# Query sketches and numerators of the later chunks in 32x32 tiles, in an attention and GELU kernel

## The chip, the core and the metric

The kernel runs on one core of a Trainium2 chip. The metric is the device time of one launch in microseconds (us): 259.41 us, the median of three runs from 259.04 to 259.57.

## What is computed

Polysketch attention (4 batches, 4 heads, 1088 tokens, head width 32) feeds a feed-forward layer with exact GELU. All in float32; `moe_w_in` and `moe_w_out` come as float64.

```python
def phi(x):                                   # S1, S2: (8, 32)
    a = np.einsum('rd,bhsd->bhsr', S1, x)
    b = np.einsum('rd,bhsd->bhsr', S2, x)
    return np.einsum('bhsi,bhsj->bhsij', a, b).reshape(*x.shape[:-1], r * r)   # 64 features
q_p, k_p = phi(q), phi(k)
kv = np.einsum('bhsf,bhsd->bhfd', k_p, v)
z = np.sum(k_p, axis=2)
num = np.einsum('bhsf,bhfd->bhsd', q_p, kv)
den = np.einsum('bhsf,bhf->bhs', q_p, z)[..., None] + 1e-06
x = (num / den)                               # then (B*S, H*D) = (4352, 128)
h = x @ w_in                                  # (4352, 2048)
out = (0.5 * h * (1 + erf(h / sqrt(2)))) @ w_out
```

## The kernel before

**Chunks.** The 1088 tokens of a batch are two chunks of 512 and a remainder of 64. Chunks 0 to 7 are the full ones (`n // 2` is the batch), and chunk 8 holds the four remainders, 256 tokens. For each chunk the attention output stands as `xT` (128 channels by 512 tokens). From it PE (TensorE) makes 16 blocks of hidden channels (`hidden`, L721), ACT (ScalarE) applies GELU (L728), and PE multiplies with `w_out`: most of it in `two_products` (L807), a seven-product scheme whose sums of tokens POOL (GpSimd) makes; some directly in `project` (L858, L855).

**Order.** The order is written out by hand. A table of steps `t` has one hidden block per step (16 per full chunk; chunk `n` begins at `t = 16 n`); `at(t, f, ...)` puts a piece of attention into a step, and within a step an engine does its instructions in the order of the text. Chunk `n`'s query is sketched at the step before chunk `n - 1`'s hidden blocks begin, and its numerators are made one chunk later, at the step before its own hidden blocks begin. Chunks 6, 7 and 8 go together at the end (`last_sketches`, `last_attends`).

**The query path of chunks 2 to 8** (chunks 0 and 1 go another way and are not changed):

- `query_turn` (DVE, VectorE) turns the query so that partitions are head and channel: `qT`.
- `query_sketch` (L578) multiplies `qT` with the sketch matrices on PE. `S_abc[b]` holds, for a batch, four columns of `S1`, four of the sketch of `z` and eight of `S2`, for each of two heads. One product contracts 64 rows (two heads, with zeros in the foreign part of the weights), has 32 columns of weights and streams 256 tokens. Eight products make a chunk: two pairs of heads (row groups of 64), two halves of the features and two halves of the tokens (four column groups of 32).
- `query_outer` (DVE, L590 to L613) turns the result in 32x32 blocks, adds up the denominator, which lies in two groups of partitions (four reductions at L601 swap them), takes its reciprocal, multiplies out the 64 features and turns them back: `q_pT`.
- `attend_products` (L633): numerators, 64 features by 32 channels, eight products of 256 tokens. `kz[b]` holds key-times-value of batch `b`, twice, once for each half of the partitions.
- `take_x` (ACT, L644): one copy of the numerators to `xT`.

**The key path of a batch.** `features_of_all` (L977) and `outer_of_all` make key features, `add_tokens` sums them; `z_sum` and `kv_sum` (both L437) multiply on PE; `fold_z` puts the sketch of `z` into `S_abc` (DVE, L492 to L495); `turn_kv` (L467) turns key-times-value with a product for each half of the partitions, and ACT copies it to `kz` (L468). `repeat_first_z` and `turn_first_kv` do the same for batch 0, whose copy for the remainder is `kz_first` (L503).

**PSUM.** The pool `wps` has two buffers of two banks (`w_ps`). `work_banks()` takes one buffer, and a piece that takes one waits for the last use of what stood there. In `sketch_and_attend` a sketch and numerators share a pair and the key features have the other; in `kv_and_attend` and `last_sketches` the pieces take pairs one after the other.

**DMA.** All loads and nearly all stores are issued from one queue, SP's, in the order of the text: the loads, `q_rem` (L128, 16 transfers) last, then the stores of the output (L878, L884).

Of the kernel before, what the change touches and what calls it, by code (L numbers as in the profile page):

```python
# [16 lines left out]
def kernel(  # L17
# [210 lines left out]
    kz = [big.tile([128, 128], FP, name=f"kz{b}") for b in range(B)]  # L228

    kz_first = big.tile([128, 128], FP, name="kz_first")  # L230
# [218 lines left out]
    def z_sum(b):  # L449

        held["z"] = work_bank()
        for h in range(H):
            kv_product(held["z"], ones, k_s[b][:, h], h, 0, start=True, stop=True)
# [10 lines left out]
    def turn_kv(b, banks):  # L464

        for rows in (slice(0, 64), slice(64, 128)):
            pe.matmul(banks[rows, 1, :128], lhsT=kv_T[b], rhs=ident, start=True, stop=True)  # L467
        act.copy(out=kz[b], in_=banks[:, 1, :128])  # L468
# [3 lines left out]
    S_abc = [big.tile([128, 2, 2, 2 * R], FP, name=f"S_abc{b}") for b in range(B)]  # L472
    own_r = big.tile([128, 2], FP, name="own_r")

    def spread_sketches():

        pool.tensor_add(out=own_r, in0=mask4[:, 0:2], in1=mask4[:, 2:4])
        own = own_r[:, None, :, None]
        w = S_abc[0]
        pool.memset(w, 0.0)  # L480
        pool.tensor_mul(out=w[:, :, :, 0:4], in0=sT[:, 0:R].rearrange("p (i f) -> p i f", i=2)[:, :, None].broadcast_to([128, 2, 2, 4]),
                        in1=own.broadcast_to([128, 2, 2, 4]))
        pool.tensor_mul(out=w[:, :, :, R:], in0=sT[:, None, None, R:].broadcast_to([128, 2, 2, R]),
                        in1=own.broadcast_to([128, 2, 2, R]))
        pool.tensor_mul(out=S_ab, in0=sT[:, None].broadcast_to([128, 2, 2 * R]), in1=own_r[:, :, None].broadcast_to([128, 2, 2 * R]))
        for b in range(1, B):
            pool.tensor_copy(out=S_abc[b], in_=w)

    def sketch_of_z(b, ps, at):

        zs = att.tile([128, R, R], FP, name="z_s")
        dve.tensor_mul(out=zs, in0=ps[:, at:at + F].rearrange("p (i j) -> p i j", i=R), in1=sT[:, None, R:].broadcast_to([128, R, R]))  # L492
        c = ps[:, 2 * F:2 * F + R]
        dve.tensor_reduce(out=c, in_=zs, axis=mybir.AxisListType.X, op=AX.add)
        dve.tensor_mul(out=S_abc[b][:, :, :, 4:8], in0=c.rearrange("p (i f) -> p i f", i=2)[:, :, None].broadcast_to([128, 2, 2, 4]),  # L495
                       in1=own_r[:, None, :, None].broadcast_to([128, 2, 2, 4]))

    def repeat_first_z():

        of = kz[0].rearrange("f (r x) -> f r x", r=2)  # L500
        to = kz_first.rearrange("f (c r d) -> f c r d", c=NP, r=2)
        for c in range(NP):
            act.copy(out=to[:F, c], in_=of[c * F:(c + 1) * F, :, 0:D])  # L503
# [57 lines left out]
    def batch_of(n, s, i):  # L561
        return n // NCH if n < NMAIN else i * 2 + s
# [3 lines left out]
    def query_sketch(n, ps=None, tok=None):  # L566

        ps = work_banks() if ps is None else ps
        W = width[n]
        tok = ps[:, :, CW // 2:] if tok is None else tok  # L570
        m = 1 if n < NMAIN else B // 2
        N = W // 2 // m
        for s in range(2):
            for i in range(m):
                for fh in range(2):
                    for c in range(NP):
                        rows, q4 = slice(c * 64, (c + 1) * 64), 2 * s + fh
                        pe.matmul(ps[q4 * 32:(q4 + 1) * 32, c, i * N:(i + 1) * N],  # L578
                                  lhsT=S_abc[batch_of(n, s, i)][rows, fh].rearrange("p r x -> p (r x)"),
                                  rhs=qT[n].rearrange("p h j t -> p (h j t)")[rows, (s * m + i) * N:(s * m + i + 1) * N],  # L580
                                  start=True, stop=True)
        sketched[n] = ps, tok

    def query_outer(n):

        W = width[n]
        K, H2 = W // 16, W // 2
        ps, tok = sketched.pop(n)
        tok = tok[:, :, :H2]
        dve.transpose(out=tok, in_=ps[:, :, :H2])  # L590
        x = tok.rearrange("p c (k x) -> p c k x", x=2 * R)
        a, b = x[:, :, :, 0:4], x[:, :, :, 8:16]
        m = att.tile([128, 32, 4], FP, name="q_ac")[:, :K]
        den = att.tile([128, 32], FP, name="q_den")[:, :K]
        by_c = lambda t: t.rearrange("p (c k) i -> p c k i", c=NP)
        dve.tensor_copy(out=by_c(m), in_=x[:, :, :, 4:8])
        dve.tensor_mul(out=by_c(m), in0=a, in1=by_c(m))
        part = ps[:, 0, :K]
        dve.tensor_reduce(out=part, in_=m, axis=mybir.AxisListType.X, op=AX.add)
        for g in range(4):  # L600
            dve.tensor_reduce(out=den[(g ^ 1) * 32:((g ^ 1) + 1) * 32], in_=m[g * 32:(g + 1) * 32], axis=mybir.AxisListType.X,  # L601
                              op=AX.add)
        dve.scalar_tensor_tensor(out=den, in0=part, scalar=1e-6, in1=den, op0=AX.add, op1=AX.add)
        dve.reciprocal(out=den, in_=den)
        dve.tensor_mul(out=by_c(m), in0=a,
                       in1=den.rearrange("p (c k) -> p c k", c=NP)[:, :, :, None].broadcast_to([128, NP, K // 2, 4]))
        feat = att.tile([128, 2 * CW], FP, name="q_f", bufs=1)[:, :2 * W]
        qp[n] = att.tile([128, 2, W], FP, name="q_pT" if n < NMAIN else "q_pT_rem", bufs=2 if n < NMAIN else 1)
        for c in range(NP):
            dve.tensor_mul(out=feat[:, c * W:(c + 1) * W].rearrange("p (k i j) -> p k i j", i=4, j=R),  # L610
                           in0=by_c(m)[:, c, :, :, None].broadcast_to([128, K // 2, 4, R]),
                           in1=b[:, c, :, None, :].broadcast_to([128, K // 2, 4, R]))
# [4 lines left out]
    def attend(n, banks=None):  # L617
        attend_products(n, banks)
        take_x(n)

    def attend_products(n, banks=None):


        W = width[n]
        m = 1 if n < NMAIN else B // 2
        banks = work_banks() if banks is None else banks
        f = qp[n].rearrange("f r x -> f (r x)")[:, :2 * W].rearrange("f (c i n r t) -> f c i n r t", c=NP, i=m, r=2, t=32)
        N = W // 2 // m
        for i in range(m):
            for s in range(2):  # L630
                rows, b = slice(s * 64, (s + 1) * 64), batch_of(n, s, i)
                for h in range(H):
                    pe.matmul(banks[h * D:(h + 1) * D, s, i * N:(i + 1) * N],  # L633
                              lhsT=(kz[b] if b else kz_first)[rows, h * D:(h + 1) * D],
                              rhs=f[rows, h // 2, i, :, h % 2], start=True, stop=True)
        numerators_in[n] = banks

    def take_x(n):

        W, banks, m = width[n], numerators_in.pop(n), 1 if n < NMAIN else B // 2  # L640
        xT[n] = att.tile([128, CW], FP, name="xT", bufs=3)
        to = xT[n][:, :W]
        to = to.rearrange("p (s x) -> p s x", s=2) if m == 1 else to.rearrange("p (s t i) -> p s i t", s=2, i=m)
        act.copy(out=to, in_=banks[:, :, :W // 2] if m == 1 else banks[:, :, :W // 2].rearrange("p s (i t) -> p s i t", i=m))  # L644
# [326 lines left out]
    def features_of_all(b):  # L971

        ps = work_banks()
        for g in range(4):
            for c in range(NP):
                rows = slice(c * 64, (c + 1) * 64)
                pe.matmul(ps[g * 32:(g + 1) * 32, c, :CW // 2], lhsT=S_ab[rows].rearrange("p r x -> p (r x)"),  # L977
                          rhs=kT[g // 2][rows, g % 2 * 256:(g % 2 + 1) * 256], start=True, stop=True)
        held["keys"] = ps

    def outer_of_all(b):

        ps = held["keys"]
        tok = ps[:, :, CW // 2:]
        dve.transpose(out=tok, in_=ps[:, :, :CW // 2])
# [11 lines left out]
    def add_tokens(b):  # L997

        sums = held["keys"][:, :, :2 * F]
# [11 lines left out]
    def sketch_and_attend(n):  # L1011

        ps = work_banks()
        query_sketch(n, ps)
        attend(n - 1, ps[:, :, CW // 2:])

    def last_sketches(b):

        z_sum(b)
        fold_z(b)  # L1020
        banks = work_banks()
        kv = banks[:, 1, CW // 2 + 128:]
        kv_sum(b, kv)
        attend_products(NMAIN - 3, banks)
        query_sketch(NMAIN, banks[:, :, CW // 2:], banks)
        take_x(NMAIN - 3)
        take_kv(b, kv)
        two = work_banks()
        query_sketch(NMAIN - 2, two, banks)
        query_sketch(NMAIN - 1, two[:, :, CW // 2:], two)  # L1030
        query_outer(NMAIN)

    def last_attends():

        banks = work_banks()
        attend_products(NMAIN - 2, banks)
        attend_products(NMAIN - 1, banks[:, :, CW // 2:])
        attend_products(NMAIN)
# [9 lines left out]

    def kv_and_attend(b, n):

        banks = held["kv"] = work_banks()
        kv_sum(b, banks[:, 1, CW // 2:])
        if n >= NCH:
            attend(n, banks)
        take_kv(b, banks[:, 1, CW // 2:])
# [17 lines left out]
    at(16, features_of_all, 1)  # L1073
# [6 lines left out]
    at(24, z_sum, 1)  # L1080
    at(24, fold_z, 1)
    at(23, query_turn, 3)
    at(24, kv_and_attend, 1, 1)
    at(24, query_sketch, 2)
# [6 lines left out]
    for n in range(3, NCHUNK):  # L1091
# [4 lines left out]
        if n == NMAIN - 2:  # L1096
# [5 lines left out]
            at(t + 11, lambda b=b: turn_kv(b, work_banks()))  # L1102
# [5 lines left out]
        if keys:  # L1108
            at(t - 1, sketch_and_attend, n)
            at(t - 1, features_of_all, b)  # L1110
        else:
            if n % 2 == 0 and b < B:
                at(t - 1, z_sum, b)
                at(t - 1, fold_z, b)
# [139 lines left out]
```

## Time and profile before

| | |
|---|---|
| median of three runs | 259.41 us (259.04 to 259.57) |
| profiled execution, first to last instruction (span) | 257.9 us |
| granted TensorE clock, mean | 0.999 |
| L721, hidden products (64 or 128 columns of weights) | 514 passes, 136.9 us busy |
| L807, output products | 784 passes |
| L578 sketches, 256 columns / 64 columns | 96 / 32 passes |
| L633 numerators, 256 columns / 64 columns | 96 / 32 passes |
| DVE, one query step L590 to L613 (pack at 57.40) | 6.4 us |
| ACT, one copy to `xT` (L644, 128x512) | 0.59 us |

The profile is one execution, so durations are set against its span; the time of that execution is not listed by itself, and the median of the runs lies 1.5 us above the span. In a row of the timeline the first number is the start in us from the first instruction, the second the length, then engine, line of the kernel, operation, tiles (out<-in), shape and count. A float32 matmul stands in the trace as two passes, so a count of 16 is eight matmuls. In brackets stands how long the engine had been idle and what released it. The ends of matmuls are modelled, so starts are the safer number.

### The profile page before, as it was taken

What the parts mean: (1) busy time and instruction counts of PE and PEld (TensorE: products, weight loads), DVE (VectorE), ACT (ScalarE), POOL (GpSimd) and SP (SyncE); (2) the same over time, 40 slices, a digit from 0 to 9 for tenths busy, and PEclk for the clock granted to TensorE, in tenths of its full rate; (3) what the DMA queues carried; (4) which work ended last, traced back from release to release, by engine and by line L of the source; (5) the groups of instructions that cost most, each with busy time, mean ns of one, the idle gap of its engine ahead of it and who ended that gap; (6) DMA issues with size and microseconds to landing.
All of it is one profiled execution on the core that took longest, in us unless ns stands there. A gap on an engine that the chain in (4) does not pass through costs nothing.

```text
span 257.9 us, 5770 instructions
## 1 busy us (share of the span) xinstructions
PE 253.1 (98%) x2335; PEld 135.5 (53%) x2335; DVE 151.1 (59%) x313; ACT 115.2 (45%) x224; POOL 163.6 (63%) x173
## 2 busy tenths in 40 slices
PE   8989999999999999999999999999999999999995
PEld 7846444354444545444444455455544444445794
DVE  3786888969699997590178986399307000700330
ACT  4665777433626332543335332533444334433442
POOL 3313006799968778587758775787758777877300
PEclk9999999999999999999999999999999999999999
DMA  6459747751000101102000002000200200020020
GB/s 203 143 156 375 181 117 174 211 131 15 4 0 13 29 3 23 20 8 35 3 0 3 0 10 37 0 1 3 41 3 5 38 0 1 7 36 0 3 41 20
DMA packets 29594, 13.48 MB, mean 52 GB/s; under 512 B 21888, under 2 KB 27776, under 8 KB 29568
## 3 DMA queue, kind: packets, MB, share of 16 engines
q1 hardware_dynamic: 29392, 13.05, 20.2%
q8 instruction: 18, 0.29, 0.5%
q10 hardware_dynamic: 176, 0.07, 0.1%
q14 instruction: 8, 0.07, 0.1%
HBM read 10.88 MB, written 2.23 MB: 51 GB/s over the span
## 4 chain that ended last, share of the span: by engine, by line
PE 93%; SPq 2%; DMA 2%; DVE 1%; issue 0%; ACT 0%
PE h_ps L721 45%; PE o_ps L807 33%; PE o_ps L858 5%; PE w_ps L855 3%; DMA small<-in_moe_w_in_dram 2%; PE w_ps L437 1%; PE w_ps L578 1%; PE w_ps L633 1%; SPq L132 1%; PE h_ps L737 1%; SPq L100 1%; PE w_ps L977 1%; PE w_ps L656 0%; SPq L118 0%; PE w_ps L467 0%
## 5 line engine op out<-in xcount | busy, mean ns | idle before, releaser
L721 PE MATMUL h_ps<-xT,w_in 128*64 128x512 f32 (+3 forms) x514 | 136.9, 576 | 0.0
L728 ACT ACTIVATE block<-h_ps 128x512 f32<-128x512 f32 (+1 forms) x128 | 73.1, 571 | 117.2 <-PE h_ps L721 115.3
L721 PEld LDWEIGHTS h_ps<-xT,w_in 128*64 128x64 f32 (+1 forms) x514 | 41.9, 142 | 30.5 <-issue 11.6
L807 PE MATMUL o_ps<-block,w_out 128*64 128x256 f32 x224 | 57.5, 379 | 0.0
L772 POOL TENSOR_TENSOR bits_low<-block 128x512 f32<-128x512 f32 x28 | 36.0, 1286 | 27.7 <-ACT block L728 27.7
L807 PEld LDWEIGHTS o_ps<-block,w_out 128*64 128x64 f32 x224 | 30.5, 137 | 38.0 <-issue 27.5
L773 POOL TENSOR_TENSOR bits_a<-block 128x512 f32<-128x512 f32 x28 | 35.8, 1278 | 11.8 <-ACT block L728 11.8
L822 DVE COPY sums<-o_ps 64x256 f32<-64x256 f32 x8 | 3.3, 417 | 60.6 <-PE o_ps L807 60.6
L774 POOL TENSOR_TENSOR bits_e<-bits_a,block 128x512 f32<-128x512 f32 x28 | 36.1, 1288 | 2.2
L775 POOL TENSOR_TENSOR bits_m<-block,bits_e 128x512 f32<-128x512 f32 x28 | 35.9, 1282 | 2.2
L807 PE MATMUL o_ps<-bits_a,small 128*64 128x256 f32 x112 | 28.8, 379 | 0.0
L807 PE MATMUL o_ps<-bits_low,small 128*64 128x256 f32 x112 | 28.8, 379 | 0.0
L807 PE MATMUL o_ps<-block,small 128*64 128x256 f32 x112 | 28.8, 379 | 0.0
L807 PE MATMUL o_ps<-bits_m,w_out 128*64 128x256 f32 x112 | 28.7, 379 | 0.0
L807 PEld LDWEIGHTS o_ps<-block,small 128*64 128x64 f32 x112 | 15.2, 137 | 17.9 <-issue 10.8
L807 PE MATMUL o_ps<-bits_e,small 128*64 128x256 f32 x112 | 17.0, 383 | 0.0
L858 PE MATMUL o_ps<-g,w_out 128*128 128x512 f32 (+1 forms) x34 | 16.5, 572 | 0.0
L807 PEld LDWEIGHTS o_ps<-bits_m,w_out 128*64 128x64 f32 x112 | 15.3, 137 | 0.0
L807 PEld LDWEIGHTS o_ps<-bits_a,small 128*64 128x64 f32 x112 | 15.2, 137 | 0.0
L807 PEld LDWEIGHTS o_ps<-bits_low,small 128*64 128x64 f32 x112 | 15.2, 137 | 0.0
L590 DVE STREAM_TRANSPOSE w_ps<-w_ps 128x512 f32<-128x512 f32 (+1 forms) x7 | 4.8, 687 | 17.1 <-ACT xT L644 12.7
L807 PEld LDWEIGHTS o_ps<-bits_e,small 128*64 128x64 f32 x112 | 7.7, 137 | 10.6 <-issue 8.8
(195 smaller groups left out, 303.7 us busy)
## 6 DMA issues: line engine op xcount, KB each, us to landing
block<-in_moe_w_in_dram SPq DMA_DIRECT2D x3, 512.0 KB, 11.3
block<-in_moe_w_out_dram SPq DMA_DIRECT2D x3, 512.0 KB, 14.7
k<-in_k_dram SPq DMA_DIRECT2D x12, 128.0 KB, 2.9
v<-in_v_dram SPq DMA_DIRECT2D x12, 128.0 KB, 3.5
q<-in_q_dram SPq DMA_DIRECT2D x24, 64.0 KB, 2.1
out_dram<-oT SPq DMA_DIRECT2D x21, 64.0 KB, 2.2
k<-in_k_dram SPq DMA_DIRECT2D x2, 256.0 KB, 2.8
q<-in_q_dram SPq DMA_DIRECT2D x2, 256.0 KB, 3.9
```

The lines of the kernel that those rows point to most:

```text
L100: eng.dma_start(out=main[n, b][:, heads], in_=src_of[n][b, heads, 0:MAIN, :].rearrange("h (p j) d -> p h j d", j=J))
L590: dve.transpose(out=tok, in_=ps[:, :, :H2])
L721: pe.matmul(ps[rows, :W], lhsT=w[:, rows], rhs=xT[n][:, :W], start=True, stop=True)
L728: act.activation(out=g_of[n, fi][:, :W], in_=ps[:, :W], func=ACT.Gelu)
L772: pool.tensor_sub(out=s[3], in0=a11, in1=a21)
L773: pool.tensor_add(out=s[1], in0=a21, in1=a22)
L774: pool.tensor_sub(out=s[2], in0=s[1], in1=a11)
L775: pool.tensor_sub(out=s[4], in0=a12, in1=s[2])
L807: pe.matmul(acc[n][bank][half * 64:(half + 1) * 64, col:col + HW], lhsT=fixed, rhs=moving, start=opens and e == 0 and name in "4715", stop ...
L822: dve.tensor_copy(out=N[lo, 0, one], in_=a0[lo, one])
L855: pe.matmul(o_of[n][i][:, :128], lhsT=g[:, i * 128:(i + 1) * 128], rhs=w_tile(w_out_sb, fi), start=first, stop=final)
L858: pe.matmul(o_of[n][:, cols], lhsT=w_tile(w_out_sb, fi), rhs=g[:, cols], start=first, stop=final)
```

## The change

A sketch product now contracts the 32 rows of one head, with the weights `S_acb[b]` (128x32: eight columns of `S1`, eight for the sketch of `z`, eight of `S2`, eight of zeros), and streams a quarter of the tokens: 16 products of 128 columns, head by row group and token quarter by column group, each head into a bank of its own. So all 64 features of a token come out on the same partitions; the denominator is one reduction, and `query_outer` loses the four reductions, the zeros and a multiplication. A head's 64 features then lie in two blocks of 32 (`i`), so the numerators are 32 products of 128 columns that add up in pairs. `kz[b]` is `[128, 2, 128]`: `turn_kv` makes one product, ACT copies its two halves to the first 32 partitions, and three DMAs on SP spread them to the other three groups. `take_x` makes two copies, one for each pair of banks. Sketch, numerators and key features (or `z`, key-times-value and its turned form) now share four banks that are taken together.

The core of the diff (changed names in calls, and the remainder's index forms in part, left out):

```diff
-    def turn_kv(b, banks):
-        for rows in (slice(0, 64), slice(64, 128)):
-            pe.matmul(banks[rows, 1, :128], lhsT=kv_T[b], rhs=ident, start=True, stop=True)
-        act.copy(out=kz[b], in_=banks[:, 1, :128])
+    def turn_kv(b, ps):
+        pe.matmul(ps[:F, :128], lhsT=kv_T[b], rhs=ident, start=True, stop=True)
+        for i in range(2):
+            act.copy(out=kz[b][:32, i], in_=ps[i * 32:(i + 1) * 32, :128])
+        for g in range(1, G):
+            sp.dma_start(out=kz[b][g * 32:(g + 1) * 32], in_=kz[b][:32])
...
-    S_abc = [big.tile([128, 2, 2, 2 * R], FP, name=f"S_abc{b}") for b in range(B)]
+    S_acb = [big.tile([128, 4 * R], FP, name=f"S_acb{b}") for b in range(B)]
...
     def repeat_first_z():
...
         for c in range(NP):
-            act.copy(out=to[:F, c], in_=of[c * F:(c + 1) * F, :, 0:D])
+            for i in range(2):
+                act.copy(out=to[:, i, c], in_=of[c * F + i * 32:c * F + (i + 1) * 32, :, 0:D])
...
+    def bank_pairs():
+        return work_banks(), work_banks()
...
-    def query_sketch(n, ps=None, tok=None):
...
-        for s in range(2):
-            for i in range(m):
-                for fh in range(2):
-                    for c in range(NP):
-                        rows, q4 = slice(c * 64, (c + 1) * 64), 2 * s + fh
-                        pe.matmul(ps[q4 * 32:(q4 + 1) * 32, c, i * N:(i + 1) * N],
-                                  lhsT=S_abc[batch_of(n, s, i)][rows, fh].rearrange("p r x -> p (r x)"),
...
+    def query_sketch(n, two, lo):
+        q_cols = qT[n].rearrange("p h j t -> p (h j t)")
+        N = width[n] // G
+        for g in range(G):
+            for h in range(H):
+                rows = slice(h * D, (h + 1) * D)
+                pe.matmul(two[h // 2][g * 32:(g + 1) * 32, h % 2, lo:lo + N], lhsT=S_acb[batch_of(n, g)][rows],
+                          rhs=q_cols[rows, group_cols(n, g)], start=True, stop=True)
...
     def query_outer(n, ...):
...
-        dve.transpose(out=tok, in_=ps[:, :, :H2])
+        for c in range(NP):
+            dve.transpose(out=tok[:, c].rearrange("p (r x) -> p r x", r=2), in_=two[c][:, :, lo:lo + N])
...
-        part = ps[:, 0, :K]
-        dve.tensor_reduce(out=part, in_=m, axis=mybir.AxisListType.X, op=AX.add)
-        for g in range(4):
-            dve.tensor_reduce(out=den[(g ^ 1) * 32:((g ^ 1) + 1) * 32], in_=m[g * 32:(g + 1) * 32], ...)
-        dve.scalar_tensor_tensor(out=den, in0=part, scalar=1e-6, in1=den, op0=AX.add, op1=AX.add)
+        dve.tensor_reduce(out=den, in_=m, axis=mybir.AxisListType.X, op=AX.add)
+        dve.tensor_scalar(out=den, in0=den, scalar1=1e-6, scalar2=None, op0=AX.add)
...
+    def attend_products(n, two, lo):
+        N = width[n] // G
+        f = qp[n].rearrange("f r x -> f (r x)").rearrange("f (h k i t) -> f h k i t", h=H, i=2, t=32)
+        for i in range(2):
+            for g in range(G):
+                rows, b = slice(g * 32, (g + 1) * 32), batch_of(n, g)
+                for h in range(H):
+                    pe.matmul(two[g // 2][h * D:(h + 1) * D, g % 2, lo:lo + N],
+                              lhsT=(kz[b][rows] if b else kz_first)[:, i, h * D:(h + 1) * D],
+                              rhs=f[rows, h, :, i], start=i == 0, stop=i == 1, skip_group_check=True)
...
+        for c in range(NP):                       # take_x
...
+            act.copy(out=to, in_=two[c][:, :, lo:lo + N])
...
+    def sketch_and_attend(n, b):
+        two = bank_pairs()
+        query_sketch(n, two, 0)
+        attend_products(n - 1, two, 128)
+        features_of_all(b, two[1][:, :, CW // 2:], two[1][:, :, :CW // 2])
+        take_x(n - 1)
+
+    def kv_and_sketch(b, n):
+        two = bank_pairs()
+        held["z"], kv = two[0][:, 0, CW // 2:], two[1][:, 1, CW // 2:]
+        held["kv"] = two[1][:, 1, CW // 2 + 128:]
+        z_sum(b)
+        fold_z(b)
+        kv_sum(b, kv)
+        if n > NCH:
+            attend_products(n - 1, two, 128)
+        query_sketch(n, two, 0)
+        if n > NCH:
+            take_x(n - 1)
+        take_kv(b, kv)
+
+    def last_sketches(b):
+        two = bank_pairs()
...
+        attend_products(NMAIN - 3, two, 320)
+        query_sketch(NMAIN, two, 256)
+        query_sketch(NMAIN - 2, two, 0)
+        query_sketch(NMAIN - 1, two, 128)
         take_x(NMAIN - 3)
         take_kv(b, kv)
+        query_outer(NMAIN, 320)
 
     def last_attends():
-        banks = work_banks()
-        attend_products(NMAIN - 2, banks)
-        attend_products(NMAIN - 1, banks[:, :, CW // 2:])
-        attend_products(NMAIN)
+        two = bank_pairs()
+        for i, n in enumerate(range(NMAIN - 2, NCHUNK)):
+            attend_products(n, two, i * 128)
         for n in range(NMAIN - 2, NCHUNK):
             take_x(n)
...
-            at(t + 11, lambda b=b: turn_kv(b, work_banks()))
+            at(t + 11, lambda b=b: turn_kv(b, work_bank()))
```

## The prediction

> **What bounds the kernel now.** I read the page first: shares of the span, then the chain that ended last.
>
> ```profile
> PE 253.1 (98%) x2335; PEld 135.5 (53%) x2335; DVE 151.1 (59%) x313; ACT 115.2 (45%) x224; POOL 163.6 (63%) x173
> ...
> PE 93%; SPq 2%; DMA 2%; DVE 1%; issue 0%; ACT 0%
> ```
>
> PE is the bound from about 15 us to the end, at a granted clock of 0.999, so a nanosecond counts only if PE's stream gets shorter or has to wait. DVE, ACT and POOL have room: the 1.15 us of four reductions that each query loses on DVE is worth nothing by itself.
>
> The changed work sits in six short packs on PE, from 56.6 to 184.3 us. I then read the timeline of PE and ACT around the packs. In pack 4, which sets up chunk 3 (start and length in us, engine, line, operation):
>
> ```profile
> 98.89 0.66 PE L633 MATMUL w_ps<-q_pT,kz 64*32 64x256 f32 x16
> 99.34 0.64 PE L578 MATMUL w_ps<-qT,S_abc 64*32 64x256 f32 x16
> ...
> 99.66 0.59 ACT L644 COPY xT<-w_ps 128x512 f32<-128x512 f32 x1 [1.31 <-PE w_ps L633]
> ...
> 99.91 0.65 PE L807 MATMUL o_ps<-bits_e,small 128*64 128x256 f32 x4
> ...
> 100.39 0.60 PE L721 MATMUL h_ps<-xT,w_in 128*64 128x512 f32 x2
> ```
>
> Every product counts twice in these rows (two passes for f32). Eight tiles run together, and from start to start a set of 8 passes takes 0.216 us, so 8 products cost 0.43. The numerators (L633) come first; ACT's copy to `xT` runs beside the sketch (L578) and ends at 100.25, and the first hidden product (L721) needs it at 100.39. That margin of 0.14 us is what the reader should keep in mind. The last pack:
>
> ```profile
> 182.86 1.09 PE L633 MATMUL w_ps<-q_pT,kz 64*32 64x256 f32 x32
> 183.75 0.24 PE L633 MATMUL w_ps<-q_pT_rem,kz_first 64*32 64x64 f32 x4
> 183.78 0.24 PE L633 MATMUL w_ps<-q_pT_rem,kz 64*32 64x64 f32 x4
> 183.81 0.24 PE L633 MATMUL w_ps<-q_pT_rem,kz_first 64*32 64x64 f32 x4
> 183.83 0.51 PE L633 MATMUL w_ps<-q_pT_rem,kz 64*32 64x64 f32 x20
> ...
> 184.06 1.07 ACT L644 COPY xT<-w_ps 128x512 f32<-128x512 f32 x2 [0.49 <-PE w_ps L633]
> ...
> 184.27 0.65 PE L807 MATMUL o_ps<-bits_e,small 128*64 128x256 f32 x4
> ...
> 184.75 0.60 PE L721 MATMUL h_ps<-xT,w_in 128*64 128x512 f32 x2
> ```
>
> Here the copy of chunk 6 starts at 184.06, before the remainder's products are through, ends at 184.65, and L721 follows at 184.75.
>
> **The price of a small product.** The change turns 8 products of 256 columns on 8 tiles into 16 of 128 on 16 tiles (sketch), and 8 into 32 (numerators: each head's 64 features now lie in two blocks of 32 that are added up). By columns alone a set of 16 passes lasts half of 0.216, so a sketch falls from 0.43 to 0.22 and the numerators stay at 0.43. But then passes must start 6.8 ns apart without end. Does the trace show that? The nearest row is the remainder's pack above: 64 columns on 8 tiles, the same density. In narrow windows of the timeline its first 17 passes start 7 ns apart (nine products, queued while the long ones ran); then comes a hole of 75 ns, and from 183.94 on a new product only every 16.6 ns (183.944, 183.961, 183.977, 183.994, ...). All 16 take 373 ns, 23.3 each. So a product costs 13.6 ns at best (columns), 16.6 when it comes straight from PE's queue, 23.3 at worst. I take 16.6, because the new packs of 48 to 96 products outlast any store of nine; the ends go into the range.
>
> The Trainium skill ("TensorE: Matmul & The Clock Gate", section "Wait — 56ns, not 53.3ns?") says that matmuls never start closer than about 25 ns. The rows show four passes on four tiles within 27 ns, so here the floor holds at most for one tile; by the page's figure the last pack's 192 passes alone would need 4.8 us, an estimate. The same page's Part 3 gives about 4 ns between tiles that run together, against 6.8 here; by it only the first price would be left.
>
> **Who waits for the pack.** The copies to `xT` were one per chunk and are now two of 128x256, one for each pair of banks. An ACT copy of that size takes 0.37 (L703) and follows its neighbour with 0.10 overlap (the two above take 1.07, 0.59 each): 0.64 for both. The waits written into the changed program say what they wait for. In packs 4 and 6 the copies now stand behind the sketches, whose products lie in the same banks; in packs 3 and 5 the second copy waits for the key features, which moved into the second pair; in the last pack both wait for all 96 products, where the copy used to wait for the first 16. After the last pass start come 0.27 for a pass of 128 columns (L467: 272 ns; 0.22 for 64), 0.11 from PE to ACT (99.55 to 99.66), the copies, and 0.10 back to PE (taken equal to the way there). On PE, L807 takes only 0.48 of that in packs 4, 5, 6 and the last, and the switch to it 0.14.
>
> **The sum, pack by pack** (13.6 / 16.6 / 23.3 ns; start of the next thing on PE against before):
>
> - Pack 2: one sketch, no `xT`. 16 products 0.22 / 0.27 / 0.37 for 0.43: -0.21 / -0.16 / -0.06.
> - Pack 3: 48 products 0.65 / 0.80 / 1.12 for 0.86. L721 comes 1.3 us later, so the copy is covered: -0.21 / -0.07 / +0.26.
> - Pack 4: 98.89 + 48 products + 0.27 + 0.11 + 0.64 + 0.10 = 100.66 / 100.81 / 101.13 for 100.39: +0.27 / +0.42 / +0.74.
> - Pack 5: the second copy waits for the features (two sets, the last pass 0.27 after the first, 0.38 long): 126.10 + 48 products + 0.27 + 0.38 + 0.11 + 0.37 + 0.10 = 127.98 / 128.13 / 128.45 for 128.04: -0.06 / +0.09 / +0.41.
> - Pack 6: 32 numerators, 16 for the remainder, 32 for two sketches: 154.78 + 80 products + 1.12 = 156.99 / 157.23 / 157.76 for 157.16: -0.17 / +0.07 / +0.60.
> - Last pack: 182.86 + 96 products + 0.22 + 0.11 + 0.64 + 0.10 = 185.24 / 185.52 / 186.17 for 184.75: +0.49 / +0.77 / +1.42.
>
> Sum: +0.1 / +1.1 / +3.4 us. From the middle I take off 0.1, for about nine products per pack that lie ready at 13.6. That gives +1.0.
>
> **Edits that cost nothing, and their cover.** `turn_kv` drops one of two products that ran side by side: nothing either way. Its two ACT copies of 32 partitions replace one of 0.26; ACT then sits idle for 0.8 us or more, and the four copies of `repeat_first_z` (0.49 for two before) fit into 0.68. The nine new DMAs: for `kz1` they stand on SP behind the 16 loads of `q_rem`, which end at 64.1; at 0.4 to 0.5 per issue and 1.7 to landing (the `q_rem` row) the last lands at 67.2, and PE wants it at about 68.6. At the 3.5 of the v loads it would be 69.0, and PE would stand 0.4. `kz2` stands behind 16 stores until 106.3 and is wanted at 126; `kz3` is written at about 177.3, lands by 180.7 and is wanted at 182.8. The last `turn_kv` (176.09) now waits for the second transpose of chunk 7's query on DVE, behind the drain (ends 168.74) and chunk 6's query: 6.4 us less 1.15 and what the narrower steps save, plus 0.2 for the split transpose, so it is through at about 174.9. Without these 1.2 us PE would stand for what is missing. Behind the query steps on DVE nothing comes later than before.
>
> **Rivals.**
> - *PE's queue keeps up* (13.6 ns): for it the 7 ns at the pack's head; against it the 16.6 after nine products. +0.1: 259.5, no change to be seen.
> - *Sixteen tiles go badly* (23.3 ns or worse, or kz late): for it the whole remainder pack, and no row with 16 tiles; against it that the hole came once only. +3.4: 262.8; half way, 261.6.
> - *Faster: the wait for `xT` does not bind.* If the copies start when the numerators are done, as before, only PE's stream counts. At 13.6 it is -0.21 in each of packs 2 to 5, 1.09 for 1.75 in pack 6 (-0.66), 1.31 for 1.27 in the last: -1.5, 257.9. It decides in packs 4 and 6 and the last, once copies start before the last sketch ends and the pace is under about 15 ns. Against it stand the waits in the program.
>
> **How the numbers follow.** The profiled execution's span is 257.9 us; the median of the runs, 259.41, is 1.5 above it, and I let that stand. +1.0 gives 260.4. Chances: forecast (259.9 to 261.4) 0.50; queue keeps up 0.22; tiles go badly 0.18; faster 0.10. The range from 259.2 to 262.2 leaves out the faster case and the worst of the bad one. A measurement tells about 0.2% (0.5 us) from no change: faster 0.10, same 0.22, slower 0.68.
>
> **What would show it.** In the timeline after: the last pack lasting about 1.6 us, with L721 at least 0.3 behind the end of L807 in pack 4 and the last, and ACT's `xT` copies starting after the last small product. L721 directly behind L807 there would prove the waits wrong; packs of 0.65 (pack 3) and 1.3 us (last) would prove the pace wrong; PE standing before the first numerators would be kz.

## The result, and the profile after

The changed kernel takes 266.39 us (median of six runs, 264.75 to 267.47), the kernel before 259.38 beside it: ratio 1.026 (95% interval 1.024 to 1.028). The forecast was 260.4, at most 262.2: right that it is slower, wrong by 6 us. The profiled execution has a time of 265.60 and a span of 263.8 against 257.9. From the page of the changed kernel:

```profile
PE 257.6 (98%) x2745; PEld 158.6 (60%) x2745; DVE 145.8 (55%) x288; ACT 117.2 (44%) x236; POOL 163.3 (62%) x173
...
q8 instruction: 21, 0.34, 0.6%
...
PE 97%; issue 1%; ACT 0%
```

DVE does 5 us less, and it is worth nothing: PE is still the chain. PE has 410 passes more (2745 for 2335). In the chain "issue", time in which PE waits for nothing that the profile shows, has grown from 0 to 1%. I had no term for it. The instruction queue made 21 loads of 16 KB, 18 before.

Where did 5.9 us come from? I took the start of every hidden product (L714, before L721; they run in pairs, and I took the later one of each) and subtracted its start before. Between the packs the difference stands still to 0.01 us; it jumps at the packs:

| | forecast, us | measured, us |
|---|---|---|
| pack 2 (one sketch) | -0.16 | -0.19 |
| pack 3 | -0.07 | +0.55 |
| pack 4 | +0.42 | +0.73 |
| pack 5 | +0.09 | +0.72 |
| pack 6 | +0.07 | +2.48 |
| last pack | +0.77 | +1.46 |
| the rest | 0 (-0.1 on all packs) | +0.10 |
| sum | +1.0 | +5.85 |

Four timelines of PE and ACT show how. Columns: start, length in us, engine, line, operation, operands, passes. Pack 3 after:

```profile
68.27 0.50 PE L578 MATMUL w_ps<-qT,S_acb 32*32 32x128 f32 x32
...
68.59 1.17 PE L621 MATMUL w_ps<-q_pT,kz 32*32 32x128 f32 x64
...
69.69 0.66 PE L969 MATMUL w_ps<-kT,S_ab 64*32 64x256 f32 x16
```

From the first sketch to the key features (L969) it is 1.42 us, where 0.89 stood before and I had taken 0.80: 1.22 from first to last pass start of the 48 products, and 0.20 more until the features start on their 64x32 tiles. For that 0.20 I had no term; pack 5 is alike. Pack 4 after:

```profile
99.35 0.96 PE L621 MATMUL w_ps<-q_pT,kz 32*32 32x128 f32 x57
...
100.16 0.67 PE L578 MATMUL w_ps<-qT,S_acb 32*32 32x128 f32 x30
100.76 0.65 PE L800 MATMUL o_ps<-bits_e,small 128*64 128x256 f32 x4
100.83 0.65 ACT L637 COPY xT<-w_ps 128x256 f32<-128x256 f32 x2 [2.03 <-PE w_ps L578]
...
101.53 1.08 PE L714 MATMUL h_ps<-xT,w_in 128*64 128x512 f32 x4
```

The copies to `xT` start when the sketches end, not the numerators, and L714 comes 0.77 behind L800 (0.48 before): the wait that I had forecast. But the 48 products need 1.22 us from first to last pass start, where I had taken 0.80. Pack 6 after:

```profile
157.94 0.98 PE L578 MATMUL w_ps<-qT,S_acb 32*32 32x128 f32 x59
158.94 0.37 ACT L637 COPY xT<-w_ps 128x256 f32<-128x256 f32 x1 [2.79 <-PE w_ps L578]
...
160.74 0.29 PE L578 MATMUL w_ps<-qT,S_acb 32*32 32x128 f32 x1 [1.82 <-issue]
160.96 0.65 PE L800 MATMUL o_ps<-bits_e,small 128*64 128x256 f32 x4
```

One last pass of the sketches comes 1.82 us behind all others. No semaphore, engine or data holds it. The last pack after:

```profile
187.24 1.79 PE L621 MATMUL w_ps<-q_pT,kz 32*32 32x128 f32 x121
...
189.40 0.45 PE L621 MATMUL w_ps<-q_pT_rem,kz 32*32 32x64 f32 x20
189.71 1.25 ACT L637 COPY xT<-w_ps 128x256 f32<-128x256 f32 x4 [1.75 <-issue]
...
190.47 0.65 PE L714 MATMUL h_ps<-xT,w_in 128*64 128x512 f32 x2
```

It is 2.54 us up to L800 (1.40 before; the forecast was 1.59 for the products and 0.14 for the switch to L800), and L714 0.20 later behind it than before. So there are three things to test: the gap, the price of a product, and the wait for `xT`.

### The profile page after: what moved, and what is told of

Same layout as the page of the kernel before. It is cut to its first block, busy times and chain, and to the rows that moved or that the text cites. A ratio compares the mean times of both kernels' runs of the same rounds, so it can differ in the third digit from the quotient of the medians.

```text
span 263.8 us, 6589 instructions
## 1 busy us (share of the span) xinstructions
PE 257.6 (98%) x2745; PEld 158.6 (60%) x2745; DVE 145.8 (55%) x288; ACT 117.2 (44%) x236; POOL 163.3 (62%) x173
## 4 chain that ended last, share of the span: by engine, by line
PE 97%; issue 1%; ACT 0%
PE h_ps L714 44%; PE o_ps L800 32%; PE o_ps L851 5%; PE w_ps L848 3%; PE w_ps L621 2%; PE w_ps L437 1%; PE w_ps L883 1%; PE w_ps L578 1%; PE w_ps L539 1%; PE o_ps L426 1%; PE h_ps L730 1%; PE w_ps L969 1%; PE w_ps L649 0%; PE h_ps L333 0%; PE w_ps L333 0%
## 5 line engine op out<-in xcount | busy, mean ns | idle before, releaser
L714 PE MATMUL h_ps<-xT,w_in 128*64 128x512 f32 (+3 forms) x514 | 142.2, 577 | 0.2
L721 ACT ACTIVATE block<-h_ps 128x512 f32<-128x512 f32 (+1 forms) x128 | 73.1, 571 | 114.4 <-PE h_ps L714 114.1
L714 PEld LDWEIGHTS h_ps<-xT,w_in 128*64 128x64 f32 (+1 forms) x514 | 49.8, 143 | 25.2 <-issue 10.5
L800 PE MATMUL o_ps<-block,w_out 128*64 128x256 f32 x224 | 57.6, 379 | 0.0
L800 PEld LDWEIGHTS o_ps<-block,w_out 128*64 128x64 f32 x224 | 30.5, 137 | 27.2 <-issue 19.8
L800 PE MATMUL o_ps<-bits_low,small 128*64 128x256 f32 x112 | 28.9, 381 | 0.0
L800 PE MATMUL o_ps<-bits_m,w_out 128*64 128x256 f32 x112 | 28.8, 380 | 0.0
L800 PE MATMUL o_ps<-bits_a,small 128*64 128x256 f32 x112 | 28.8, 380 | 0.0
L800 PE MATMUL o_ps<-block,small 128*64 128x256 f32 x112 | 28.8, 379 | 0.0
L800 PEld LDWEIGHTS o_ps<-block,small 128*64 128x64 f32 x112 | 15.2, 137 | 13.8 <-issue 8.4
L589 DVE STREAM_TRANSPOSE w_ps<-w_ps 128x256 f32<-128x256 f32 (+1 forms) x14 | 6.2, 443 | 22.2 <-ACT xT L637 18.6
L800 PE MATMUL o_ps<-bits_e,small 128*64 128x256 f32 x112 | 18.4, 383 | 0.0
L800 PEld LDWEIGHTS o_ps<-bits_a,small 128*64 128x64 f32 x112 | 15.2, 137 | 1.7 <-issue 0.3
L800 PEld LDWEIGHTS o_ps<-bits_m,w_out 128*64 128x64 f32 x112 | 15.3, 137 | 1.3
L800 PEld LDWEIGHTS o_ps<-bits_low,small 128*64 128x64 f32 x112 | 15.1, 137 | 0.8
L800 PEld LDWEIGHTS o_ps<-bits_e,small 128*64 128x64 f32 x112 | 9.7, 137 | 8.3 <-issue 6.3
```

The costliest lines, as they stand in the source:

```text
L589: dve.transpose(out=tok[:, c].rearrange("p (r x) -> p r x", r=2), in_=two[c][:, :, lo:lo + N])
L714: pe.matmul(ps[rows, :W], lhsT=w[:, rows], rhs=xT[n][:, :W], start=True, stop=True)
L721: act.activation(out=g_of[n, fi][:, :W], in_=ps[:, :W], func=ACT.Gelu)
L800: pe.matmul(acc[n][bank][half * 64:(half + 1) * 64, col:col + HW], lhsT=fixed, rhs=moving, start=opens and e == 0 and name in "4715", stop ...
```

## The experiments

### The gap of 1.82 us: PE's instructions run out

Around the point where PE stops in pack 6 (158.92 to 160.74), a 16 KB load runs on the instruction queue (158.02 to 159.32 in the trace). Every product is four PE instructions here, a weight load and a pass, twice; 21 loads of 16 KB for 5520 PE instructions come to 62 bytes each and 263 per load, which I read as 64 and 256. Theory: a pack takes instructions faster than the loads bring them. Then moving all later instructions against the loads must move the gap. Before the first keys arrive I put extra products on zeros:

```diff
+    def extra_products(n):
+        w, x = (nc.const_aps.tensor(0.0, [128, m], FP) for m in (32, 64))
+        for i in range(n):
+            pe.matmul(bank[i % 4 * 32:(i % 4 + 1) * 32, CW - 64:], lhsT=w, rhs=x, start=True, stop=True)
     bank = work_bank()
-    keep_busy(3, bank)
+    keep_busy(2, bank)
     keep_busy(1, bank, 64)
+    extra_products(57)      # shift64 and before_shift64: 17
```

**shift224.** 

> The changed kernel with one product fewer in PE's warm-up and 57 small ones more (64 columns of zeros, 4 tiles in turn), all before the first keys arrive: 224 more PE instructions ahead of everything, nothing else. Theory (instruction supply): in the changed kernel PE stands 1.82 us inside pack 6, in the middle of the sketches, without a semaphore to wait for, while a load of 16 KB on the instruction queue is under way; such loads come once for about every 256 PE instructions, so moving all later instructions by 224 (32 short of one load) moves the place where PE can run dry out of the pack. The gap of 1.82 goes and no other comes: span about 262.0 against 263.8, time 264.3 or less against 266.4. Rival (the gap belongs to the products: a tile, a bank or the copy that reads it): the gap stays at the same product, span 263.8, time 266.4.

Measured: span 262.0, time 264.81 (263.77 to 265.15), ratio to before 1.0215 (1.0194 to 1.0235). The gap is gone; the end of pack 6 is now

```profile
158.07 1.00 PE L578 MATMUL w_ps<-qT,S_acb 32*32 32x128 f32 x60
159.00 0.65 PE L800 MATMUL o_ps<-bits_e,small 128*64 128x256 f32 x4
```

and pack 6 costs +0.63 against before in place of +2.48. A load runs beside pack 6 here too (158.28 to 159.71), and PE does not stop. The span came out as the theory had it, in part by luck (0.2 us more at the start, 0.15 less in the last pack); the time is 0.5 over the 264.3 I expected, since the other executions have spans of 262.7 to 263.4.

**shift64.** 

> The same with 17 small products in place of 57: 64 more PE instructions ahead of everything. Theory (instruction supply): pack 6 still runs dry (1.9 us), and the last pack, with 384 instructions in 2.4 us, now runs dry as well, about 1.9 us at 187.6: span about 265.7, time 267.5 to 268.5. Rival: the gap belongs to the products of pack 6, span 263.8, time 266.4.

Measured: 270.61 us, ratio 1.042 (1.040 to 1.045), span 268.9. Who waited for whom on PE (us in total, times, longest), and two stretches of the trace (PE's busy time first, the granted clock third from the end):

```profile
PE w_ps L578 <- issue: 2.1, 1, 2.1
PE w_ps L621 <- issue: 1.9, 1, 1.9
...
190.00:196.00 6.00, 4.01 (x119) 2.29 (x107) 0.00 (x0) 2.15 (x7) 3.22 (x3) 0.90 0.23 39
196.00:204.00 8.00, 8.00 (x50) 3.76 (x49) 0.00 (x0) 2.48 (x5) 2.61 (x3) 0.86 0.00 0
```

Both gaps came, the second in the last pack, as foretold, but near its end (191.0) and not at 187.6. The time is 2 us over the forecast: after the second gap the granted clock fell to 0.5 for 3.41 us (194.75 to 198.17), which is worth 1.7 us by an estimate (half of 3.41), and 1.0 us more than in the changed kernel came ahead of 16 us, where the extra products stand.

**before_shift64.** 

> The kernel before, with the 64 extra PE instructions ahead of everything and nothing of the change. Theory (instruction supply): counted by the loads of the other runs (a load is asked for after some 150 instructions of each 256, what follows it is there 3.9 us later, and PE runs dry 300 instructions after the asking), this shift lets the kernel before run dry in its own pack 6 as well: one gap of 0.4 to 1.9 us, 1.3 by the count, near 156; 260.3 to 261.3. Rival (only the packs of 32x32 tiles have such a gap): none, 259.4.

Measured: 261.08 us, ratio 1.0055 (1.0037 to 1.0073), span 259.7. The gap is there, in a kernel that has nothing of the change:

```profile
156.50 0.97 PE L578 MATMUL w_ps<-qT,S_abc 64*32 64x256 f32 x20
157.93 0.63 PE L578 MATMUL w_ps<-qT,S_abc 64*32 64x256 f32 x7 [0.46 <-issue]
158.49 0.65 PE L807 MATMUL o_ps<-bits_e,small 128*64 128x256 f32 x4
```

It is at the low end (0.46 where the count said 1.3), and pack 6 ends 1.0 us later than before: from pass start to pass start the hole is 0.84, of which the modelled end of the pass before it leaves 0.46. Another 0.8 us of this run came ahead of 16.1 us, at the start, where the extra products stand; it says nothing on the theory, and without it the time would stand at the lower edge of the 260.3 to 261.3.

What settles it is a count. I numbered all PE instructions in the runs that have a gap, seven with bench. PE stops behind number 3777 in the changed kernel, behind 3777 and 4545 in shift64, 3777 and 4545 in before_split, 3521 in half, 3777 in orders, 5057 in bench (these four below), 3265 in before_shift64. Each of these nine is a multiple of 256 plus 193: PE stops at the same place in a block, whatever product stands there. That the stops belong to the instruction blocks is thereby shown; why at the 193rd, no run shows.

### The price of a product

**before_split.** The rest of the loss could lie in the number of products or in the sixteen small tiles. So I gave the kernel before as many products as the changed one, on its own tiles:

```diff
+        P = 2 if n < NMAIN else 1                 # query_sketch
-        for s in range(2):
+        for e, s in ((e, s) for e in range(P) for s in range(2)):
...
+        P = 4 if n < NMAIN else 2                 # attend_products
-        for i in range(m):
+        for e, i in ((e, i) for e in range(P) for i in range(m)):
```

Each product then takes the columns from `e * N / P` to `(e + 1) * N / P`.

> The kernel before, with its own 64-row tiles, its own waits and all its DVE work, but each sketch product cut into 2 of 128 columns, each numerator product into 4 of 64 columns (the remainder's numerators into 2 of 32): as many small products as in the changed kernel, the same columns in all, one tile after the other in rounds of 8. Theory (what costs is the number of products, four PE instructions each): packs 3 and 5 last about 1.3 us from the first sketch to the key features against 0.89 before, the last pack about 2.2 to L807 against 1.40, pack 6 may run dry (up to 1.9 us); the sum is +2 to +4.5 us, 261.5 to 264. Rival (sixteen tiles of 32x32 are what is slow): the sets keep their 0.43, nothing is lost, 259.4.

Measured: 265.49 us, ratio 1.0235 (1.0214 to 1.0255), nearly as much as the change loses, with none of its tiles, but not by the same terms. Packs 3, 4 and 5 cost +0.29, +0.27 and +0.29 (I had expected 0.4 in packs 3 and 5), the last +0.76 (2.17 us to L811), pack 6 +2.73, of which 2.19 is a gap at "issue":

```profile
156.74 1.07 PE L580 MATMUL w_ps<-qT,S_abc 64*32 64x128 f32 x53
160.00 0.42 PE L580 MATMUL w_ps<-qT,S_abc 64*32 64x128 f32 x7 [2.19 <-issue]
```

A second gap of 1.22 stands behind the last pack (L725 comes 1.8 late by it); it is what lifts the time over the 264 that I expected. So the two gaps make some 4.0 of the 6.3 us in this run's span, and the number of products some 2.2; the changed kernel loses some 4.0 without its gap. The 16 sketches of 128 columns on 8 tiles lost nothing (8 passes every 0.109 us, as by columns); the 32 numerators of 64 columns took 0.69 in pack 3, where 0.43 of columns stood. So the number costs, once columns are too few to hide it. The changed kernel loses 0.26 to 0.46 more per pack than this one in packs 3 to 5, of which the wait for `xT` is 0.29 in pack 4 and 0.12 in pack 5. Some of the rest is the 0.20 up to the key features in packs 3 and 5: here they start among the last numerators, with no such pause (pack 3: 69.55, the last numerators at 69.61).

**bench.** This measures the price by itself:

```diff
+    def price(pair, rows, cols, n, dt=FP):
+        for i in range(n):
+            g, h = (i // 4 % 4, i % 4) if rows == 32 else (i // 4 % 2, i % 4)
...
+            pe.matmul(pair[g // 2][h * 32:(h + 1) * 32, g % 2, :cols], lhsT=w, rhs=x, start=True, stop=True)
```

`w` and `x` are zeros of 32 and of `cols` columns on the rows of group `g`.

> The changed kernel with six series of 48 small products on zeros ahead of its work, each behind eight wide products; only the series are read, the time of the whole means nothing. 16 tiles of 32x32 with 128, 64 and 16 columns, 8 tiles of 64x32 with 128 and 16 columns, and 16 tiles with 128 columns in bf16 (one pass instead of two). Theory (a product costs PE's queue 16.6 ns, for two weight loads and two passes, and each return to the first tile holds the queue for about one pass): first to last pass 1.15 us, 0.95 and 0.80 on 16 tiles, 1.3 (the columns themselves) and 0.8 to 0.9 on 8, and half, 0.4 to 0.6, in bf16, which has half of the instructions. Rival (columns and tiles set the price): 0.65, 0.33 and 0.1 on 16 tiles, 1.3 and 0.2 on 8, 0.33 in bf16. A second rival (32x32 tiles are slow in themselves): the 16-column series on 16 tiles costs much more than that on 8.

The series in the timeline:

```profile
6.01 1.49 PE L889 MATMUL w_ps<-const-float32-0.0 32*32 32x128 f32 x96
11.11 1.17 PE L889 MATMUL w_ps<-const-float32-0.0 32*32 32x64 f32 x96
15.89 0.99 PE L889 MATMUL w_ps<-const-float32-0.0 32*32 32x16 f32 x96
20.49 1.61 PE L889 MATMUL w_ps<-const-float32-0.0 64*32 64x128 f32 x96
25.71 1.00 PE L889 MATMUL w_ps<-const-float32-0.0 64*32 64x16 f32 x96
30.31 0.60 PE L889 MATMUL w_ps<-nought_b 32*32 32x128 bf16 x48
```

The lengths include the last pass. From first to last pass start it is 1.220, 0.955, 0.814, 1.339, 0.817 and 0.377 us. With 16 columns, 48 products take 0.81 on 16 tiles as on 8: 17 ns each, so this floor is set neither by the tile's size nor by the columns. In bf16, with half of the instructions, it is less than a third of the first series, a little under the 0.4 to 0.6 expected (this number alone would also fit the columns, 0.33). The first series, on zeros, with no data to wait for, lasts 1.220; pack 4 of the changed kernel lasts 1.218. Nothing but the products is needed to explain these 1.22. Between 16 and 128 columns lie 0.41 us. In the first series the first round over the 16 tiles takes 0.32 us, the second 0.47 and the third 0.44 (0.23, 0.31 and 0.28 with 16 columns): PE is slower once products come back to a tile. Part of that are holes, of 85 and 111 ns at the first return and 49 at the second. Why they stand there I can't tell.

**half.** Only `i = 0` of the two halves is left:

```diff
-        for i in range(2):                        # attend_products
+        for i in range(1):
```

> The changed kernel without the second half of the numerators (the products of features 32 to 63 are left out): 16 products a chunk in place of 32. Theory (after its first round of 16 products a pack pays about 0.48 us for each further round): packs 3, 4 and 5 lose 0.48 each, the last pack three rounds of less, 1.2 to 1.4. Rival (columns set the price, 0.22 for a round): 0.2 to 0.25 a pack, 0.6 in the last. Where the instruction loads fall is another matter in this run, so the packs are to be compared and not the time.

Measured in the packs, up to the next work on PE: -0.42 in packs 4 and 5, -1.23 in the last. So a further round of 16 costs 0.42, 26 ns a product, not 0.48, and twice what columns say. Pack 3 fell by only 0.11, because in this run SP issued the loads of `q_rem` late, the last piece of `kz1` landed at 69.7, and PE waited 0.2 for it. In the profiled run of the changed kernel the second piece was there at 65.1.

**orders.** The loops of a round in another order: `h` outside `g` in pack 3, `(g, (g + d) % 4)` in pack 5, `i` inside in pack 4.

> The changed kernel with the same products in another order: in pack 3 the row group changes from product to product (heads in the outer loop), in pack 4 the two halves of a numerator follow each other on the same tile, in pack 5 row group and column group change both (diagonals); pack 6 and the last pack as they are. Theory (the price is that of a round over the 16 tiles, whatever its order): packs 3 and 5 last 1.41 us from the first sketch to the key features as before, within 0.05. Rival (neighbours in the order that share a row group or a bank hinder each other): packs 3 and 5 fall towards 1.0. In pack 4 both expect no gain: by a queue that lets others pass 1.4, by one that holds everything behind a busy tile up to 3 us more.

Measured from the first sketch to the key features: 1.415 in pack 3 and 1.414 in pack 5, within 2 ns of what they were (1.417 and 1.415). Neighbours in the order don't matter. In pack 4, with the two halves one after the other on a tile, the products took 1.82 up to L800 in place of 1.41: the queue holds what is behind a busy tile, but not for all of its time.

### The wait for xT

**pairs.** The sketches (and key features) go first, the numerators last, those of the first two banks ahead of the others, so that the first copy runs beside the rest:

```diff
+        todo = [(i, g) for p in range(2) for i in range(2) for g in (2 * p, 2 * p + 1)]
...
+        query_sketch(n, two, 0)                   # kv_and_sketch
         attend_products(n - 1, two, 128)
-        query_sketch(n, two, 0)
         take_x(n - 1)
```

> The changed kernel with the 224 extra instructions ahead (no gap in pack 6), and in packs 3 to 6 the sketches and key features first and then the numerators, first those of the first pair of banks, then those of the second: the first copy to xT waits for half of the numerators only, and runs beside the rest. Theory (in packs 4 and 5 the first hidden product waits for both copies, each 0.37, behind the last product): L714 comes 0.3 us earlier behind the last product in pack 4, 0.5 behind L800's start; pack 5 the same; against it rounds of 8 tiles instead of 16, up to 0.1 us a pack. Sum -0.3 to -0.6 us against 264.8. Rival (something else holds the first hidden product, the PE queue or the switch of tiles): no gain in packs 4 and 5.

Measured: 264.16 us in one run, span 262.3 (shift224: 262.0). Pack 4 in this run:

```profile
100.42 1.25 PE L623 MATMUL w_ps<-q_pT,kz 32*32 32x128 f32 x64
101.29 0.79 ACT L639 COPY xT<-w_ps 128x256 f32<-128x256 f32 x2 [1.73 <-PE w_ps L623]
101.60 0.65 PE L802 MATMUL o_ps<-bits_e,small 128*64 128x256 f32 x4
...
102.13 1.08 PE L716 MATMUL h_ps<-xT,w_in 128*64 128x512 f32 x4
```

The first copy now runs beside the products and the first hidden product follows L802 by 0.53 in place of 0.77: the wait was what I said. But it pays little. Against shift224 packs 4 and 6 gain 0.16 and 0.18, packs 3 and 5 lose 0.15 and 0.08, though pack 5 was to gain like pack 4. Rounds of 8 tiles return sooner, and in packs 3 and 5 the sets change tile shape once more; that these are the reasons was not tested. The sum over the packs, the last included, is -0.09, short of the -0.3 to -0.6 that I expected; the span is 0.4 longer all the same, as 0.5 more stands at the start.

### One product for the transpose

**before_turn1.** Behind each `turn_kv` the changed kernel was 0.16 us earlier. Could the kernel before have that?

```diff
-        for rows in (slice(0, 64), slice(64, 128)):
-            pe.matmul(banks[rows, 1, :128], lhsT=kv_T[b], rhs=ident, start=True, stop=True)
-        act.copy(out=kz[b], in_=banks[:, 1, :128])
+        pe.matmul(banks[:F, 1, :128], lhsT=kv_T[b], rhs=ident, start=True, stop=True)
+        for rows in (slice(0, 64), slice(64, 128)):
+            act.copy(out=kz[b][rows], in_=banks[:F, 1, :128])
```

> The kernel before, with one of the two products of the kv transpose left out; ACT copies the one result to both halves of kz (two copies of 64 partitions in place of one of 128). In the changed kernel PE came 0.16 us earlier behind each of the three transposes, since the one product runs beside a product of the other half. Theory: the same here, 3 x 0.16 = 0.48 us, 258.9. Rival: the second ACT copy (about 0.26 us) makes kz late for the numerators or ACT late for a hidden block, 259.4 or more.

Measured: 259.43 us, ratio 1.0003 (0.9991 to 1.0015): nothing. That is the rival's time, but not for its reason. The first rows behind the transpose:

```profile
60.63 0.27 PE L466 MATMUL w_ps<-ident,kv_T 128*64 128x128 f32 x1
60.64 0.43 PE L807 MATMUL o_ps<-bits_low,small 128*64 128x256 f32 x1
60.74 0.27 PE L466 MATMUL w_ps<-ident,kv_T 128*64 128x128 f32 x1
60.85 0.38 PE L807 MATMUL o_ps<-block,small 128*64 128x256 f32 x1
```

The hidden and output products go in pairs, one on each half of PE's columns. The transpose now takes one half only, so that the other runs ahead by 0.16, and stays ahead. The next pack needs both halves and waits for the later one. Against the kernel before the leading half goes from -0.10 to -0.26 at the transpose, and back to -0.10 behind pack 3; so it does at all three. The changed kernel does the same, which is why the table goes by the later half.

No run here points to a version that is faster than the kernel before.

## Why the prediction failed, step by step

- **What bounds the kernel; DVE's saving worth nothing:** right. 5 us less on DVE, and no start on PE came earlier for it.
- **Price of a small product:** the step that failed first. I let 16.6 stand for a pack, and called 23.3, the whole remainder pack, the worst. 16.6 is about what a product costs with 16 columns (17 in the bench); with 128 columns the rounds behind the first are slower, 0.44 to 0.47 for 16 products. Measured: 1.22 for 48 products (25.4 each) where I had 0.80, and 2.40 for 96 in the last pack (187.24 to 189.64) where I had 1.59. So even the 23.3 was too low. The one row of a full small-tile pack was the nearest row after all; I had taken the smooth part of it.
- **From the small tiles to the key features:** a term put at nothing. In packs 3 and 5 I counted the products alone; 0.20 more lies between the last pass start and the features, so that the miss there is 0.62 and 0.63, of which the products make 0.42.
- **A gap for instructions:** no step at all, and the largest miss in one place, 1.82 us in the profile; the other misses of packs 3 to 6 and the last make some 2.8 together. The trace of before had the makings: 16 KB loads on the instruction queue, one for every 256 PE instructions, and packs to which the change adds up to 256.
- **Who waits for the pack:** right in kind. The copies do stand behind the sketches and the features, and L714 comes 0.29, 0.12 and 0.20 later behind L800 in pack 4, pack 5 and the last. The constants were somewhat large: from the last pass start in pack 4 it is 0.97 to L714, not 1.12, as ACT starts with the pass's end and PE 0.05 after ACT's.
- **Pack 2:** right (-0.19 for -0.16): its 16 products start within 0.25 us (0.27 forecast); one round alone has no return to a busy tile.
- **Costless edits:** right, the transpose too, though the profile looked otherwise for a while. `kz` came in time in the profiled run; the 0.2 us in half shows that the bound of 0.4 for it was a real one.
- **Span to time:** the median stands 2.6 above the profiled span, not 1.5 as before. Three of the six executions have spans of 265.4 to 265.7 with a mean clock of 0.992 to 0.994, the others 263.0 to 263.8 with 0.998 or 1.0. A lowered clock behind the gap, as in shift64 (mean 0.994), would fit; no trace of those three is on record.
- **Rivals:** "sixteen tiles go badly" was the right direction, for a reason that is in the main not the tiles, and its +3.4 was short of the +5.85.

In the bench 96 passes of 16 columns started 8.5 ns apart. The floor of about 25 ns between starts that I had weighed (the Trainium skill, "TensorE: Matmul & The Clock Gate", "Wait — 56ns, not 53.3ns?") doesn't hold across tiles. And PE stood nine times for 0.46 to 2.19 us at the same place of an instruction block. On these loads the Trainium skill ("Runtime: NRT & Kernel Launch", "Instruction fetch mechanics") gives blocks of 16 KB and 256 instructions, which agrees with the count, and calls the fetch hidden, which a dense pack here is the exception to.

## What to carry to other kernels

Count a small matmul by its instructions, not by its columns: here four for an f32 product, 17 ns at least and 26 in a pack that goes round the tiles more than once, so splitting products into smaller tiles gives nothing back once their columns take less than that (16 sketches with 27 ns of columns each lost nothing in before_split; products with 13.6 took 25). Where a few hundred PE instructions stand close together, look for loads on the instruction queue and for idle time at "issue", and test it by shifting the instructions: a kernel can gain or lose 2 us by nothing else. A load beside the pack is not enough for a gap (shift224); where in its block the pack stands decides. Before a gain of one column half is believed, look whether both halves have it when they next meet.

## What the runs showed that I had not expected

- PE stops always behind the 193rd instruction of a block of 256; in pack 6 the load ended at 159.32 and PE went on at 160.74, 1.4 us later.
- The granted clock can fall to 0.5 for 3.41 us after PE has stood 1.9 us (shift64, at 194.75; also half at 160.14 and bench at 191.76). It didn't after 2.19 and 1.22 us in before_split, so the gap alone doesn't decide it. What fits all eleven traces is idle time within a window: the stretches at full clock last a whole number of times 3.41 us (21 to 76 times). If the span is cut into such windows from their bounds on, PE is idle for 1.65, 1.95 and 2.01 us in the window ahead of these three drops. The most that a window without a drop behind it has is 1.57 (the changed kernel); the 2.19 falls half into one window and half into the next. No run was made to test this, and idle times go by modelled ends.
- Twice the tiles give little: 48 products of 128 columns take 1.339 us on 8 tiles and 1.220 on 16.
